# A 3-tap convolution as transforms and matmuls: from 6 products per 4 outputs to 8 products per 6

## The chip, the cores and the metric

The kernel runs on one NeuronCore of one Trainium2 chip (trn2). The metric is device time in microseconds (us), the median of the runs of a kernel; less is better. Some runs fall in a slower state and are labelled slow (here, over 1.5% above the fastest run of the same kernel). Ratios are taken over fast runs alone; a median is over all runs given, which includes one slow run of the changed kernel and one of the experiment `e9_w0late`. The span that a profile prints is about 2 us shorter than the time reported for the same run (before the change: spans of 207.6 to 208.5 us for times of 209.4 to 210.3 us). Stages below are told in span time, totals in reported time.

Engines: PE is TensorE's matmul, PEld its weight load, DVE is VectorE, ACT is ScalarE, POOL is GpSimd, SP the engine that issues the DMAs; a q after a name (SPq, ACTq) is that engine's sequencer. PSUM is the memory that the matmuls write, in eight banks of 512 fp32 values per partition; the other tiles lie in SBUF. The drain is the end of a run, when TensorE has little left to do: in the kernel before it is counted from 203.4 us, after the last full products, in the changed kernel from the end of the last unit's tail (below), with two products still to come.

## The reference

A 1-D convolution of three taps with padding, a batch norm with given statistics, and Silu. Everything is bf16 in memory.

```python
B, S, C = 2, 2048, 1024; K = 3
xp = jnp.pad(x, ((0, 0), (1, 1), (0, 0)))
y = sum(jnp.einsum('bsc,cd->bsd', xp[:, k:k + S, :], w[k]) for k in range(K))
inv_std = 1.0 / jnp.sqrt(var + 1e-5)
y = (y - mean) * (g * inv_std) + b
return _silu(y)            # (2, 2048, 1024)
```

## The kernel before

Both kernels avoid three full matmul passes, one per tap. A block of neighbouring outputs along `s` is computed from a linear transform of its inputs (`T`), one matmul product per transformed point against transformed weights, and a linear combination of the products. Before, a block has 4 outputs and 6 products, 1.5 multiplications per output where the plain form has 3.

The input transform is itself a small matmul: a window of x (up to 128 rows of `s`) is the stationary operand and a matrix of 6 points for 31 blocks is the moving one. The result goes from PSUM to SBUF as bf16.

```python
WT = 31                                    # blocks per window
for bi in range(B):
    for wi in range(NWIN):                 # 17 windows per batch
        nc.sync.dma_start(out=xw[...], in_=x[bi, lo:hi_ld + 1, :])
        for h in range(CT // CH):
            for c4 in range(CH):
                nc.tensor.matmul(grp[:, c4, 0:6 * ntile], lhsT=xw[0:kk, ct * P:(ct + 1) * P],
                                 rhs=Rm[0:kk, :, 0:ntile], start=True, stop=True)
            # 744 elements per partition, on ScalarE or VectorE by a running balance
            ev = nc.scalar.copy(dst, src)  # or nc.vector.tensor_copy(dst, src)
```

GpSimd makes the transformed weights of one chunk of 128 output channels: six sums and two scalings of 1,024 elements per partition. There are 8 chunks.

```python
nc.gpsimd.tensor_tensor(g32, w0, w2, op=ALU.add)
nc.gpsimd.tensor_tensor(uch[:, 0], g32, w1, op=ALU.add)
nc.gpsimd.tensor_tensor(uch[:, 1], g32, w1, op=ALU.subtract)
nc.gpsimd.tensor_scalar(w2x4, w2, 4.0, 0.0, op0=ALU.mult, op1=ALU.add)
nc.gpsimd.tensor_scalar(w1x2, w1, 2.0, 0.0, op0=ALU.mult, op1=ALU.add)
nc.gpsimd.tensor_tensor(f32, w0, w2x4, op=ALU.add)
nc.gpsimd.tensor_tensor(uch[:, 2], f32, w1x2, op=ALU.add)
nc.gpsimd.tensor_tensor(uch[:, 3], f32, w1x2, op=ALU.subtract)
```

Then come 16 units (8 chunks times 2 halves of the blocks, 512 blocks each). A unit is 48 matmuls of 512 columns, 10 VectorE operations, 2 ScalarE copies and 4 Silus. Each output row of the block has a contiguous row in `yT`; a DMA transpose and four strided stores bring it out. The last unit is cut in two halves that are transposed on TensorE, to keep the end short.

```python
for gidx, j in enumerate([1, 2, 3, 4, 0, 5]):
    for ct in range(CT):
        nc.tensor.matmul(M[j], lhsT=lhsT, rhs=T_sb[:, ct, j, nsl], start=(ct == 0), stop=(ct == CT - 1))
    if j == 1:
        nc.scalar.copy(S1, M[1])
    elif j == 2:
        nc.vector.tensor_tensor(bp, S1, M[2], op=ALU.subtract)
        nc.vector.tensor_tensor(M[2], S1, M[2], op=ALU.add)
    # ... likewise for the other products, then
    # nc.scalar.activation(yT[:, i, :], src, ACT.Silu, bias=beta[...], scale=sk[...])
```

## Time and profile before

| | before |
|---|---|
| median | 209.96 us (16 runs, 209.45 to 211.96) |
| load and transform stage | until 36.9 us |
| products | 36.9 to 203.4 us |
| drain | 6.2 us |

The profile was taken in a run of 211.4 us, a little above the median. The head of its page: the span, the busy time of each engine, and then tenths busy in 40 equal slices of the span, with the granted TensorE clock and the DMA engines' share.

```profile
span 209.6 us, 3041 instructions
...
PE 194.8 (93%) x1089; PEld 105.7 (50%) x1104; DVE 130.9 (62%) x225; ACT 95.9 (46%) x142; POOL 124.1 (59%) x83
...
PE   1998698999999999999999999999999999999980
...
PEclk9999979999999999999999999999999999999996
DMA  5999970892626963695359545965694545454562
...
```

TensorE is busy 93% of the span. The first six slices are different from the rest: the DMA row is full, the PE row has holes. The view by stretches of time makes a table of it. Its columns are the stretch, its length, then the busy us (and the number of instructions) of PE, PEld, DVE, ACT and POOL, then the granted clock, the DMA share and GB/s.

```profile
...
5.00:36.90 31.90, 27.69 (x270) 24.32 (x269) 26.39 (x31) 26.53 (x37) 13.18 (x8) 0.95 0.83 270
38.00:48.35 10.35, 10.30 (x49) 4.69 (x49) 5.58 (x10) 2.69 (x4) 9.52 (x14) 1.00 1.05 154
60.00:180.00 120.00, 119.42 (x547) 54.41 (x557) 70.39 (x115) 46.31 (x69) 86.92 (x48) 1.00 0.67 135
203.40:209.60 6.20, 0.79 (x8) 0.45 (x8) 1.95 (x7) 1.64 (x4) 0.00 (x0) 0.74 0.30 70
...
```

In the third row TensorE is busy 119.4 of 120 us while VectorE is busy 70, ScalarE 46 and GpSimd 87: the middle is TensorE's. The second row is one unit of 48 matmuls in 10.35 us, so 215.7 ns each.

The groups of instructions, kept apart by shape: line, engine, operation, tiles, shape, count, then busy us and the mean ns of one.

```profile
...
L316 PE MATMUL ps_all<-T_sb,uch 128*128 128x512 bf16 x466 | 105.3, 379 | 0.9
...
L306 ACT ACTIVATE yT<-y,beta,sk 128x512 bf16<-128x512 f32 x60 | 45.6, 806 | 58.5 <-DVE y L327 46.3 <-DVE y L337 12.2
...
L155 POOL TENSOR_TENSOR uch<-g,wch 128x1024 bf16<-128x1024 f32 x8 | 17.1, 2134 | 0.2
...
L321 DVE TENSOR_TENSOR ps_all<-S,ps_all 128x512 f32<-128x512 f32 x15 | 10.3, 689 | 0.0
...
```

The mean duration of a pipelined matmul (379 ns) is not its rate (215.7 ns), so rates are read from stretches.

### The profile page before, as it was taken

How to read it: one execution, taken by the hardware profiler on the slowest of the kernel's cores; microseconds unless marked ns; L12 is line 12 of the kernel's file. 1: busy time of each engine (PE TensorE's matmuls, PEld its weight loads, DVE VectorE, ACT ScalarE, POOL GpSimd, SP SyncE). 2: the span in 40 equal slices, each digit the busy share in tenths (PEclk: the TensorE clock that was granted, in tenths of full speed). 3: DMA queues.
4: the chain of work that ended last, by engine and by line, in shares of the span. 5: the costliest groups of instructions: out<-in, count | busy, mean ns of one | idle time of the engine just before them, and what ended most of it. 6: DMA issues, size and time to landing. Idle time of an engine off the chain costs nothing.

```text
span 209.6 us, 3041 instructions
## 1 busy us (share of the span) xinstructions
PE 194.8 (93%) x1089; PEld 105.7 (50%) x1104; DVE 130.9 (62%) x225; ACT 95.9 (46%) x142; POOL 124.1 (59%) x83
## 2 busy tenths in 40 slices
PE   1998698999999999999999999999999999999980
PEld 1977587444444444444444444444444444445870
DVE  6799579355656565647474747473838383829671
ACT  3799589234343343343434342424243434343651
POOL 3030299989999999839944994299659920000000
PEclk9999979999999999999999999999999999999996
DMA  5999970892626963695359545965694545454562
GB/s 180 373 340 288 348 276 2 87 214 54 152 57 145 212 140 68 142 213 130 76 132 227 119 86 133 177 159 95 146 208 104 100 100 100 100 103 100 102 142 60
DMA packets 96035, 31.40 MB, mean 150 GB/s; under 512 B 91606, under 2 KB 91606, under 8 KB 96020
## 3 DMA queue, kind: packets, MB, share of 16 engines
q1 hardware_dynamic: 95812, 30.42, 65.1%
q0 software_dynamic: 208, 0.79, 1.5%
q8 instruction: 8, 0.13, 0.2%
q14 instruction: 7, 0.06, 0.1%
HBM read 14.95 MB, written 8.39 MB: 111 GB/s over the span
## 4 chain that ended last, share of the span: by engine, by line
PE 69%; DMA 13%; POOL 5%; DVE 4%; ACT 4%; issue 2%; SPq 1%; ACTq 0%; DVEq 0%; POOLq 0%
PE ps_all L316 64%; DMA xw<-in_x_dram 8%; PE ps_all L205 5%; DMA wch<-in_w_dram 3%; ACT T_sb L217 3%; DMA o_sb<-yT 2%; POOL f L159 1%; POOL g L154 1%; POOL uch L156 1%; POOL uch L155 1%; SPq L247 1%; DVE Rm L82 1%; ACT yT L306 1%; DVE E L68 1%; DVE y L337 1%
## 5 line engine op out<-in xcount | busy, mean ns | idle before, releaser
L316 PE MATMUL ps_all<-T_sb,uch 128*128 128x512 bf16 (+1 forms) x530 | 112.9, 366 | 0.9
L316 PEld LDWEIGHTS <-uch 128*128 128x128 bf16 x544 | 53.1, 98 | 57.6 <-issue 0.3
L306 ACT ACTIVATE yT<-y,beta,sk 128x512 bf16<-128x512 f32 (+1 forms) x68 | 49.9, 781 | 62.5 <-DVE y L327 49.9
L316 PE MATMUL ps_all<-T_sb,wch 128*128 128x512 bf16 (+1 forms) x271 | 57.8, 366 | 0.1
L316 PEld LDWEIGHTS <-wch 128*128 128x128 bf16 x272 | 26.6, 98 | 28.7
L205 PE MATMUL ps_all<-Rm,xw 126*128 126x186 bf16 (+1 forms) x272 | 28.4, 261 | 8.4 <-DVE Rm L82 4.3
L320 DVE TENSOR_TENSOR bp<-S,ps_all 128x512 f32<-128x512 f32 (+1 forms) x17 | 11.2, 656 | 37.3 <-PE ps_all L316 31.6
L205 PEld LDWEIGHTS <-xw 126*128 126x128 bf16 (+1 forms) x272 | 25.0, 106 | 11.6 <-issue 8.0
L217 ACT CAST T_sb<-ps_all 128x744 bf16<-128x744 f32 (+1 forms) x37 | 26.9, 785 | 8.1 <-PE ps_all L205 7.7
L219 DVE CAST T_sb<-ps_all 128x744 bf16<-128x744 f32 (+1 forms) x31 | 26.7, 904 | 6.2 <-PE ps_all L205 5.9
L325 DVE TENSOR_TENSOR cp<-S,ps_all 128x512 f32<-128x512 f32 (+1 forms) x17 | 11.1, 656 | 29.9 <-PE ps_all L316 29.8
L323 ACT COPY S<-ps_all 128x512 f32<-128x512 f32 (+1 forms) x17 | 9.5, 560 | 35.4 <-PE ps_all L316 35.4
L154 POOL TENSOR_TENSOR g<-wch 128x1024 f32<-128x1024 bf16 x8 | 17.0, 2123 | 12.2 <-DMA wch<-in_w_dram 11.7
L158 POOL TENSOR_SCALAR w1x<-wch 128x1024 bf16<-128x1024 bf16 x8 | 8.4, 1045 | 19.3 <-DMA wch<-in_w_dram 19.1
L159 POOL TENSOR_TENSOR f<-wch,w2x 128x1024 f32<-128x1024 bf16 x8 | 17.0, 2128 | 0.4
L155 POOL TENSOR_TENSOR uch<-g,wch 128x1024 bf16<-128x1024 f32 x8 | 17.1, 2134 | 0.2
L160 POOL TENSOR_TENSOR uch<-f,w1x 128x1024 bf16<-128x1024 f32 x8 | 17.1, 2132 | 0.2
L156 POOL TENSOR_TENSOR uch<-g,wch 128x1024 bf16<-128x1024 f32 x8 | 17.1, 2133 | 0.0
L161 POOL TENSOR_TENSOR uch<-f,w1x 128x1024 bf16<-128x1024 f32 x8 | 17.1, 2132 | 0.0
L326 DVE TENSOR_TENSOR ps_all<-S,ps_all 128x512 f32<-128x512 f32 (+1 forms) x17 | 11.2, 658 | 0.0
L321 DVE TENSOR_TENSOR ps_all<-S,ps_all 128x512 f32<-128x512 f32 (+1 forms) x17 | 11.2, 658 | 0.0
L331 DVE SCALAR_TENSOR_TENSOR y<-ps_all,bp 128x512 f32<-128x512 f32 (+1 forms) x17 | 11.1, 650 | 0.0
(34 smaller groups left out, 89.1 us busy)
## 6 DMA issues: line engine op xcount, KB each, us to landing
xw<-in_x_dram SPq DMA_DIRECT2D x30, 256.0 KB, 5.9
out_dram<-o_sb SPq DMA_DIRECT2D x60, 128.0 KB, 2.2
wch<-in_w_dram SPq DMA_DIRECT2D x21, 256.0 KB, 4.2
wch<-in_w_dram POOLq DMA_DIRECT2D x1, 768.0 KB, 11.6
out_dram<-o_sb SPq DMA_DIRECT2D x8, 64.0 KB, 1.7
xw<-in_x_dram SPq DMA_DIRECT2D x2, 252.0 KB
xw<-in_x_dram SPq DMA_DIRECT2D x2, 130.0 KB
o_sb<-yT SPq DMA_TRANSPOSE x15, 4.3
```

The costliest lines, as they stand in the source:

```text
L154: nc.gpsimd.tensor_tensor(g32, w0, w2, op=ALU.add)
L155: nc.gpsimd.tensor_tensor(uch[:, 0], g32, w1, op=ALU.add)
L156: nc.gpsimd.tensor_tensor(uch[:, 1], g32, w1, op=ALU.subtract)
L159: nc.gpsimd.tensor_tensor(f32, w0, w2x4, op=ALU.add)
L160: nc.gpsimd.tensor_tensor(uch[:, 2], f32, w1x2, op=ALU.add)
L161: nc.gpsimd.tensor_tensor(uch[:, 3], f32, w1x2, op=ALU.subtract)
L205: nc.tensor.matmul(grp[:, c4, 0:6 * ntile], lhsT=xw[0:kk, ct * P:(ct + 1) * P], rhs=Rm[0:kk, :, 0:ntile], start=True, stop=True,)
L217: ev = nc.scalar.copy(dst, src)
L219: ev = nc.vector.tensor_copy(dst, src)
L306: nc.scalar.activation(yT[:, i, :], src, ACT.Silu, bias=beta[:, dc:dc + 1], scale=sk[:, dc, i:i + 1])
L316: nc.tensor.matmul(M[j], lhsT=lhsT, rhs=T_sb[:, ct, j, nsl], start=(ct == 0), stop=(ct == CT - 1))
L320: nc.vector.tensor_tensor(bp, S1, M[2], op=ALU.subtract)
```

## The change

The change takes 6 outputs per block and 8 products: 1.33 multiplications per output instead of 1.5. A batch has 342 blocks, which is also the width of a product, so a unit is one batch of one chunk: 64 matmuls of 342 columns. There are other differences:

- The instruction order on each engine is now as written, not chosen by a scheduler.
- Batch 2's transform is interleaved with the first products, instead of coming before them.
- The scalings of the weights move to ScalarE, and one of three first sums to VectorE, from chunk 2 on. A unit's products come in three parts: the head (four), the tail (two) and the two end rows.
- The end rows (0 and 5) are accumulated in PSUM by the last two products, on top of what VectorE wrote there, and finished during the next unit.
- `yT` now holds the output in its final order, block by block with 6 elements each. So Silu writes every sixth element (end rows) or runs of four (the other rows). One DMA transpose and one 512 KB store per unit follow, with no special last unit.

```diff
-WT = 31
+R = 6
+NJ = 8
+WT = 21
+    NB = -(-S // R)                                  # 342 blocks per batch
...
+        by_dve = q == 0 and dc > 1
+        e = epool.tile([P, CT, P], FP32, name="e0" if by_dve else "e")
+        (nc.vector if by_dve else nc.gpsimd).tensor_tensor(e, a, c, op=ALU.add)
+        nc.gpsimd.tensor_tensor(u[:, 0], e, o, op=ALU.add)
+        nc.gpsimd.tensor_tensor(u[:, 1], e, o, op=ALU.subtract)
...
-                nc.tensor.matmul(M[j], lhsT=lhsT, rhs=T_sb[:, ct, j, nsl], start=(ct == 0), stop=(ct == CT - 1))
+            nc.tensor.matmul(
+                ps[:, bank, 0:NB], lhsT=lhsT, rhs=T_sb[:, ct, j, nsl],
+                start=fresh and ct == 0, stop=ct == CT - 1, skip_group_check=not fresh,
+            )
+            between()                                # batch 2's transform, 3 jobs per 2 matmuls
...
+            stt(z[:, 0], s2, -0.0125, s1)            # head: 4 products, 10 VectorE operations
+            stt(y[:, 1], s2, -0.05, s1)
+            # ... z[:, 1], y[:, 0], y[:, 2], y[:, 3] likewise
...
+            emit_product(cp, self.dc, self.bi, 5, True, between)      # tail: 2 products, 8 operations
+            pc = self.copy(cp)
+            if prev:
+                prev.silu(prev.yT[:, :, 1:5], prev.y.rearrange("p i n -> p n i"))
+            emit_product(cm, self.dc, self.bi, 6, True, between)
+            # ... d3 and s3 in PSUM, then
+            stt(s3, s3, -1.6, z[:, 0])
+            stt(d3, d3, -0.05, z[:, 1])
+            self.yT = ypool.tile([P, NB, R], BF16, name="yT")
...
+        def ends(self, between):                                      # after the next unit's head
+            emit_product(cm, self.dc, self.bi, 0, False, between)
+            self.silu(self.yT[:, :, 0], ps[:, cm, 0:NB])
+            emit_product(cp, self.dc, self.bi, NJ - 1, False, between)
+            self.silu(self.yT[:, :, R - 1], ps[:, cp, 0:NB])
...
+            nc.sync.dma_start_transpose(out=o, in_=flat)
+            nc.sync.dma_start(out=out_v[self.bi, :, :, self.dc * P:(self.dc + 1) * P], in_=o)
...
+    for i, (dc, bi) in enumerate(seq):
+        unit = Unit(dc, bi, (4, 5) if i < 2 or i % 2 else (6, 7))
+        unit.head(between, prev)
+        if prev:
+            prev.ends(between)
+        # ... weight loads and sums of chunk dc + 2
+        unit.tail(between, prev)
+        if prev:
+            prev.store()
```

## The prediction

> **What bounds the kernel now.** TensorE, in three stages. (1) Load and input transform, 4.3 to 36.9 us: the view by stretches shows the DMA share at 1.0 or more until about 30 us; the chain of waits has 16 us of x loads here. TensorE runs in pieces. (2) Products, 36.9 to 203.4 us: each stretch of 10.35 us has 48 matmuls of 512 columns and 10.30 us of busy TensorE, so 215.7 ns per matmul; 256-column ones take about 109 ns. The Trainium skill, "TensorE: Matmul & The Clock Gate", section "Wait — 56ns, not 53.3ns?", gives columns / 2.4 GHz + 2.5 ns for a warm array; this trace agrees with both. VectorE is about 60% busy, ScalarE 40%, GpSimd up to 95%. (3) Drain, 203.4 to 209.6 us.
>
> **What the change does.** It goes from 6 products per 4 outputs to 8 per 6, so 1.5 to 1.33 columns per output: 1,024 matmuls of 342 columns instead of 768 full-size ones of 512. At 342/2.4 + 2.5 = 145 ns that is 148.8 us instead of 166.5 us: 17.7 us less on the critical path. Weight loads grow from 816 to 1,024, but a 128-column load fits under 145 ns as it fits under 109 ns now.
>
> It interleaves the second batch's transform with the first products, so x loads of batch 2 are hidden. Evacuations go from 744 to 504 elements; spaced 755 ns (ScalarE) and 884 ns (VectorE) now, I estimate 555 and 634 ns. 49 per batch, 27 and 22, is about 15 us of both engines per batch. So the first batch is done at about 21 us and the second at about 37.5 us, with 33 product matmuls already done. Then 991 x 145.3 ns = 144 us brings the last product to about 182 us, if nothing else binds.
>
> **Will another engine bind?** Two units (one weight chunk) take 18.6 us of TensorE.
> - VectorE: 18 operations of 342 per unit instead of 10 of 512. Back-to-back spacing is 597 ns at 512 and 331 ns at 256, so about 420 ns at 342: 7.6 us per unit, plus about 1.2 us for a weight sum in every second unit: 16.3 of 18.6 us. Tight, but it fits.
> - GpSimd: 8 operations of 2.13 us: 17.1 of 18.6 us; the scalings move to ScalarE.
> - ScalarE: about 11 of 18.6 us.
> - Chunk 1 has the whole transform on GpSimd (22 us per chunk, starting near 9 us), ready near 56 us, just when its last products start: I allow 0 to 3 us of stall.
>
> **Worse:** the drain. No split last unit and no TensorE transposes: eight VectorE operations (3.4 us), a last product and Silu (about 2 us), then a DMA transpose (4.3 us until stores start now) and a 512 KB store (about 3.5 us). About 11.5 us after the last product's slot, against 6.2 us.
>
> **Sum.** 182 + 11.5 + about 2.5 of stalls: 196 us, range 190 to 204. Faster by over 2%: 0.88; within 2%: 0.09; slower: 0.03.
>
> **What would show it.** Product spacing near 145 ns with TensorE over 98% busy between 60 and 180 us; VectorE about 85 to 90%, GpSimd about 90% there; transform of batch 2 over by 36 to 40 us; 11 to 14 us from the last tail product to the end.
>
> **What would make it wrong.** VectorE or GpSimd binding: VectorE runs in order, and waits for copies or for the weight sum would leave TensorE waiting for its PSUM banks; GpSimd and VectorE slowing each other where both read SBUF; ScalarE's strided four-row Silu being far slower than 1.43 us; TensorE cold in the interleaved stage (at the start of this trace four 186-column matmuls take 620 ns, half speed).

## The result, and the profile after

| | before | after |
|---|---|---|
| median | 209.96 us (16 runs) | 202.67 us (11 runs, 202.13 to 205.43) |
| ratio of the fast runs | | 0.9646, 95% interval 0.9612 to 0.9681 |

A ratio is the mean time of one kernel's fast runs over that of the other's in the same rounds, so it is not quite the ratio of the medians. The change is 3.5% faster. The result lies in the predicted range of 190 to 204 us, near its upper edge, and 6.7 us above its centre of 196 us.

The first profile of the changed kernel fell on its slowest run (205.43 us, span 203.3 us). The kernel was run again unchanged, and the profile of that run (202.82 us) is the one shown and compared from here on.

> The changed kernel again, unchanged, beside the others of this call, for a profile in the fast state (the first fell in the slow one): 202 to 203.5 us, the first stages ending about 3 us earlier than in the first profile.

The repeat gave 202.81 us, ratio 0.9695 (0.9639 to 0.9751). The first transform stage and the interleaved one ended 2.6 us earlier than in the slow profile (the first stretch of uninterrupted products starts at 39.41 us, not 42.04 us); after that the two profiles run alike.

The head of its page:

```profile
span 200.7 us, 3607 instructions
...
PE 176.1 (88%) x1296; PEld 123.1 (61%) x1296; DVE 164.8 (82%) x357; ACT 148.1 (74%) x172; POOL 155.2 (77%) x85
...
PE   2599788897999999999999999999999999995800
...
DVE  5469778999797999799799999998998979797200
...
PEclk9999999999999999999999999999999999999665
DMA  5999999650059846977696679469966266453593
...
```

The view by stretches, with the same columns as before; the second row is one unit, 64 matmuls at the predicted rate:

```profile
...
5.00:39.40 34.40, 28.65 (x297) 25.10 (x296) 26.21 (x45) 27.21 (x57) 29.61 (x18) 1.00 0.99 272
60.00:69.30 9.30, 9.30 (x66) 6.21 (x64) 7.84 (x19) 7.34 (x8) 9.14 (x6) 1.00 0.95 200
60.00:180.00 120.00, 120.00 (x829) 80.20 (x827) 110.83 (x239) 97.54 (x95) 104.51 (x48) 1.00 0.72 148
183.20:200.70 17.50, 4.16 (x16) 2.09 (x15) 3.56 (x8) 7.23 (x4) 0.00 (x0) 0.67 0.58 126
...
```

In the middle TensorE is busy all of the 120 us. VectorE went from 70 to 111 of 120 us, ScalarE from 46 to 98, GpSimd from 87 to 105: the spare time of all three is much smaller, but TensorE still sets the pace. The last row is the drain: 17.5 us, where the kernel before took 6.2 us and the prediction counted 13.8 us (11.5 us after the last product's slot, which includes two products of 1.16 us).

The groups by shape:

```profile
...
L218 PE MATMUL ps<-T_sb,u 128*128 128x342 bf16 x768 | 119.1, 307 | 3.5 <-ACT T_sb L209 1.9 <-ACT yT L287 1.6
...
L287 ACT ACTIVATE yT<-y,beta,scale 128x1368 bf16<-128x1368 f32 x16 | 44.5, 2782 | 1.2 <-issue 1.2
L287 ACT ACTIVATE yT<-ps,beta,scale 128x342 bf16<-128x342 f32 x32 | 42.6, 1508 | 21.9 <-PE ps L218 20.0 <-POOL u L149 1.9
...
L150 POOL TENSOR_TENSOR u<-e,w1x 128x1024 bf16<-128x1024 f32 x16 | 37.1, 2319 | 0.0
...
L148 DVE TENSOR_TENSOR e<-wch 128x1024 f32<-128x1024 bf16 x6 | 11.4, 1896 | 0.0
...
```

The Silus stand out: 1,508 ns for 342 elements, where a Silu of 512 elements took 806 ns before. VectorE's weight sum takes 1,896 ns where the prediction had 1.2 us, and the GpSimd operations beside it 2,319 ns instead of 2,132 ns.

The chain that ended last, in order of time (start, length, what):

```profile
...
50.59 132.53 PE ps L218 x912
...
186.47 4.07 ACT yT L287 x2
190.54 1.13 ACTq L385
```

From 50.59 us to 183.12 us the chain is TensorE alone: 912 matmuls in 132.53 us, 145.3 ns each. It is the predicted rate to the digit. The chain printed ends with Silu; what follows it, the transpose and the store, is in the timeline below.

The timeline of the drain (start, length, engine, line, operation, tiles, and in brackets the idle time before it and what ended it):

```profile
...
183.21 0.52 DVE L275 TENSOR_TENSOR ps<-pc,ps 128x342 f32<-128x342 f32 x1 [1.05 <-PE ps L218]
...
185.60 4.16 PE L218 MATMUL ps<-T_sb,wch 128*128 128x342 bf16 x16 [2.50 <-DVE ps L225]
...
186.30 0.51 DVE L225 SCALAR_TENSOR_TENSOR ps<-ps,z 128x342 f32<-128x342 f32 x1
186.47 2.71 ACT L287 ACTIVATE yT<-y,beta,scale 128x1368 bf16<-128x1368 f32 x1 [1.25 <-issue]
189.07 2.60 ACT L287 ACTIVATE yT<-ps,beta,scale 128x342 bf16<-128x342 f32 x2
...
191.70 2.01 SPq L300 DMA_TRANSPOSE o<-yT  x1
196.01 0.38 SPq L301 DMA_DIRECT2D out_dram<-o  x1
```

The drain is one thing after another: VectorE 3.3 us until the Silu starts, the four-row Silu 2.6 us until the next one starts, two end rows 2.6 us, 4.3 us from the issue of the transpose to that of the store, 4.7 us from there to the end.

### The profile page after: what moved, and what is told of

Its sections match the earlier page's. It is cut to its first block, busy times and chain, and to the rows that moved or that the text cites. A ratio compares the mean times of both kernels' runs of the same rounds, so it can differ in the third digit from the quotient of the medians.

```text
span 203.3 us, 3607 instructions
## 1 busy us (share of the span) xinstructions
PE 175.3 (86%) x1296; PEld 122.3 (60%) x1296; DVE 166.7 (82%) x357; ACT 147.8 (73%) x172; POOL 153.3 (75%) x85
## 4 chain that ended last, share of the span: by engine, by line
PE 65%; ACT 2%; DVE 1%; issue 1%; ACTq 1%; DVEq 0%
PE ps L218 65%; ACT yT L287 2%; ACTq L385 1%; DVE ps L275 0%; DVE y L225 0%; DVE ps L276 0%; DVEq L385 0%; DVE ps L225 0%; DVEq L275 0%
## 5 line engine op out<-in xcount | busy, mean ns | idle before, releaser
L218 PE MATMUL ps<-T_sb,u 128*128 128x342 bf16 x768 | 119.8, 308 | 2.9 <-ACT yT L287 1.6
L218 PEld LDWEIGHTS <-u 128*128 128x128 bf16 x768 | 74.7, 97 | 38.0 <-issue 2.5
L287 ACT ACTIVATE yT<-ps,beta,scale 128x342 bf16<-128x342 f32 x32 | 42.6, 1507 | 21.9 <-PE ps L218 21.9
L287 ACT ACTIVATE yT<-y,beta,scale 128x1368 bf16<-128x1368 f32 x16 | 44.3, 2769 | 1.3 <-issue 1.3
L218 PE MATMUL ps<-T_sb,wch 128*128 128x342 bf16 x256 | 39.9, 307 | 2.5 <-DVE ps L225 2.5
L150 POOL TENSOR_TENSOR u<-e,w1x 128x1024 bf16<-128x1024 f32 x16 | 37.1, 2321 | 0.0
L201 PE MATMUL ps<-rm,xw 128*128 128x168 bf16 (+1 forms) x256 | 28.4, 258 | 9.9 <-DMA xw<-in_x_dram 5.1
L209 ACT CAST T_sb<-ps 128x504 bf16<-128x504 f32 (+1 forms) x56 | 27.2, 567 | 12.1 <-PE ps L201 11.2
L149 POOL TENSOR_TENSOR u<-e,w1x 128x1024 bf16<-128x1024 f32 x16 | 35.0, 2189 | 1.3
L211 DVE CAST T_sb<-ps 128x504 bf16<-128x504 f32 (+2 forms) x42 | 25.6, 640 | 12.0 <-PE ps L201 11.5
L225 DVE SCALAR_TENSOR_TENSOR y<-ps,y 128x342 f32<-128x342 f32 x64 | 29.7, 506 | 0.6
L149 POOL TENSOR_TENSOR u<-e,wch 128x1024 bf16<-128x1024 f32 x8 | 17.1, 2132 | 2.6 <-PE ps L218 2.4
L150 POOL TENSOR_TENSOR u<-e,wch 128x1024 bf16<-128x1024 f32 x8 | 17.1, 2133 | 0.0
```

What stands on the lines that cost most here:

```text
L149: nc.gpsimd.tensor_tensor(u[:, 0], e, o, op=ALU.add)
L150: nc.gpsimd.tensor_tensor(u[:, 1], e, o, op=ALU.subtract)
L201: nc.tensor.matmul(v[:, c], lhsT=xw[0:rows, (c0 + c) * P:(c0 + c + 1) * P], rhs=rm[0:rows, :, 0:n], start=True, stop=True)
L209: nc.scalar.copy(dst, v)
L211: nc.vector.tensor_copy(dst, v)
L218: nc.tensor.matmul(ps[:, bank, 0:NB], lhsT=lhsT, rhs=T_sb[:, ct, j, nsl], start=fresh and ct == 0, stop=ct == CT - 1, skip_group_check=not ...
```

## The experiments

All were run with three rounds beside the kernel before, on three chips: `e1`, `e3`, `e4` and `e5` in one, the repeat with `e2`, `e6` and `e7` in the next, `e8` to `e11` in the last. The changed kernel's own ratio was 0.9646 and, in its repeat, 0.9695; a difference of half a per cent is not to be read. The repeat's fast runs also spread from 202.7 to 205.0 us. So a difference of 1 to 2 us from the repeat rests on the profiles as much as on the times.

### Does Silu's strided write explain the missing time?

Theory: Silu is slow because it writes every sixth bf16 element, and this costs time only where Silu is on the chain, at unit 1's PSUM banks and in the drain. Rivals: Silu is slow for another reason, or ScalarE limits the middle too. The experiment gives a wrong result: each of the six rows is written contiguously, and the DMA transpose carries the same bytes.

```diff
-                prev.silu(prev.yT[:, :, 1:5], prev.y.rearrange("p i n -> p n i"))
+                prev.silu(prev.yT[:, 1:5, :], prev.y)
...
-            self.yT = ypool.tile([P, NB, R], BF16, name="yT")
+            self.yT = ypool.tile([P, R, NB], BF16, name="yT")
...
-            self.silu(self.yT[:, :, 0], ps[:, cm, 0:NB])
+            self.silu(self.yT[:, 0, :], ps[:, cm, 0:NB])
...
```

> Wrong result on purpose: Silu writes each of the six output rows contiguously (layout row, block) instead of every sixth element; all else, and the bytes moved, are as after the change. Theory S (the strided write makes Silu slow, and it counts only at unit 1's PSUM wait and in the drain): one-row Silu falls from 1.51 to about 0.6 us, four-row from 2.77 to about 1.45 us; TensorE's wait of 1.6 us near 52 us falls under 0.7 us, the drain shortens by about 3 us; total 3.5 to 4.5 us less, near 198.5 us. Rival (Silu is slow for another reason, PSUM source or size): durations stay, time the same. Rival (ScalarE also limits the middle): more than 6 us less.

Measured: 201.47 us, ratio 0.9577 (0.9527 to 0.9628), span 198.7 us; wrong output. The groups by shape:

```profile
...
L287 ACT ACTIVATE yT<-y,beta,scale 128x1368 bf16<-128x1368 f32 x16 | 24.5, 1530 | 2.6 <-issue 2.6
...
L287 ACT ACTIVATE yT<-ps,beta,scale 128x342 bf16<-128x342 f32 x32 | 20.3, 636 | 30.7 <-PE ps L218 30.6
...
```

The durations are as expected: 1,508 became 636 ns and 2,782 became 1,530 ns, so the layout is what makes Silu slow. For the end rows, read from PSUM in order in both kernels, it is the write alone. For the four-row Silu the edit changes two things, as its diff shows: it also reads `y` row by row instead of jumping between rows. Which of the two costs the 1.25 us there is not shown. The Trainium skill, "ScalarE: Activation LUTs", section "What ACT_TABLE_LOAD costs", gives 186 ns, plus 93 ns for each per-partition operand, plus 0.833 ns per element. With two such operands an estimate from these figures is 657 ns for 342 elements and 1,512 ns for 1,368; the contiguous form agrees within 4%, the strided one does not at all.

TensorE's wait before unit 1's tail fell from 1.63 to 0.72 us, about as expected. The middle did not move, so ScalarE does not limit it. But the drain shortened by 1.3 us (17.5 to 16.2 us), not 3, and the total by 1.3 us against the repeat (2.0 us of span between the two profiles), not 3.5 to 4.5. So the layout explains only part of the missing time. The drain's timeline shows where the rest of the gain went:

```profile
...
184.94 3.97 PE L218 MATMUL ps<-T_sb,wch 128*128 128x342 bf16 x16 [2.50 <-DVE ps L225]
...
187.42 0.64 ACT L287 ACTIVATE yT<-ps,beta,scale 128x342 bf16<-128x342 f32 x1
...
188.95 0.64 ACT L287 ACTIVATE yT<-ps,beta,scale 128x342 bf16<-128x342 f32 x1 [0.90 <-PE ps L218]
189.61 2.58 SPq L300 DMA_TRANSPOSE o<-yT  x1
...
```

The last 16 matmuls took 3.97 us, 248 ns each instead of 145, and the last Silu waited 0.90 us for them. The three Silus together became 2.4 us shorter here (5.2 to 2.8 us), and this wait took back 0.9 of it. TensorE had paused 2.5 us for VectorE, and the granted clock in the stretch from 185 to 190 us was 0.70. In the kernel as changed the same slow products are hidden behind the slow Silu (4.16 us, granted clock 0.66, from 185.60 us above). Taking one link out of a serial chain uncovered the next: TensorE running at a reduced clock.

### Is the cost per 4-byte word?

From 1,508 ns for 342 elements and 2,782 ns for 1,368 one might guess a cost per 4-byte word touched: three words for the four middle rows, one for an end row. Moving the tile by one element makes it two aligned words for the middle rows.

```diff
-            self.yT = ypool.tile([P, NB, R], BF16, name="yT")
+            self.yS = ypool.tile([P, NB * R + 2], BF16, name="yT")
+            self.yT = self.yS[:, 1:NB * R + 1].rearrange("p (n i) -> p n i", i=R)
...
```

> Correct result: the tile that Silu writes starts one bf16 element later, so that rows 1 to 4 of each block fill two aligned 4-byte words instead of touching three. Theory W (the cost is per 4-byte word touched, about 2.4 ns): four-row Silu falls from 2.77 to about 2.0 us, one-row stays 1.5 us; about 0.7 us less in all, if the DMA transpose does not mind the odd start. Theory E (the cost is per element written out of sequence): both stay, time the same.

Measured: 202.92 us, ratio 0.967 (0.9604 to 0.9735), correct. The four-row Silu took 2,762 ns, the one-row 1,506 ns: nothing moved. The word theory falls. What exactly the cost counts stays open; 0.9 us (end row) to 1.3 us (four rows) per Silu is what the layout costs.

### Does unit 1 wait for unit 0's banks?

Units 0 and 1 use the same two PSUM banks for their last products. In the repeat's timeline this is the line of TensorE that waits:

```profile
...
50.59 7.12 PE L218 MATMUL ps<-T_sb,u 128*128 128x342 bf16 x48 [1.63 <-ACT yT L287]
...
```

```diff
-        unit = Unit(dc, bi, (4, 5) if i < 2 or i % 2 else (6, 7))
+        unit = Unit(dc, bi, (6, 7) if i % 2 else (4, 5))
```

> Correct result: units take their last two PSUM banks in turn from the start, so unit 1 no longer writes the banks that unit 0's end rows still hold. Theory: TensorE's wait of 1.63 us on the one-row Silu before 53 us (a strided Silu of 1.5 us, where the prediction counted 0.6) vanishes whole, 1.3 to 1.7 us less. Rival: VectorE is busy without a gap there, so the wait only moves to a PSUM bank that VectorE holds: under 0.5 us.

Measured: 201.61 us, ratio 0.9603 (0.9576 to 0.9629), correct; the repeat of the change in the same rounds had 202.81 us and 0.9695. So 1.2 us by the medians. In its profile TensorE goes from 47.44 us to the end of unit 1 without that wait:

```profile
...
49.76 7.12 PE L218 MATMUL ps<-T_sb,u 128*128 128x342 bf16 x48
...
```

VectorE, busy without a gap in that stretch, does not take it back.

### Can the drain be cut?

The last unit alone is finished in two halves of 171 blocks, transposed on TensorE and stored in four pieces, as the kernel before did.

```diff
-    prev.silu(prev.yT[:, :, 1:5], prev.y.rearrange("p i n -> p n i"))
-    prev.ends(between)
-    prev.store()
+    prev.drain(between, CUTS)
+        def drain(self, between, cuts):
+            for lo, hi in cuts:                       # (0, 171), (171, 342)
+                self.silu(self.yT[:, lo:hi, 1:5], self.y[:, :, lo:hi].rearrange("p i n -> p n i"))
+                emit_product(cm, self.dc, self.bi, 0, False, between, lo, hi)
+                self.silu(self.yT[:, lo:hi, 0], ps[:, cm, lo:hi])
+                # ... row 5 likewise
+            for q in range(4):
+                for k in range(4):
+                    nc.tensor.transpose(v[:, k], flat[:, (4 * q + k) * P:(4 * q + k + 1) * P], ident)
+                # ... copy to o, store a quarter
```

> Correct result: the last unit alone is finished in two halves of 171 blocks, transposed on TensorE and stored in four pieces, instead of whole rows, a DMA transpose and one 512 KB store. Theory (the drain of 17.5 us is a serial chain after the last tail product: VectorE 3.3, four-row Silu 2.7, end rows 2.6, DMA transpose 4.3, store 4.5 us): the drain falls to 11.5 to 13 us, 4.5 to 6 us less. Rival (the end is held by what is still in the DMA queues, unit 14's transpose and store): under 2 us.

Measured: 199.38 us, ratio 0.95 (0.9474 to 0.9526), correct: 3.4 us less than the repeat. The drain is 14.5 us (183.3 to 197.8 us). This is less than expected. The timeline offers one reason, which the run after the next tests: TensorE started the first half's end rows only when VectorE was nearly done with the second half, and then ran at a granted clock of 0.66 to 0.70.

```profile
...
187.02 4.22 PE L221 MATMUL ps<-T_sb,wch 128*128 128x171 bf16 x32 [3.81 <-DVE ps L228]
...
```

With the banks in turn as well:

> Correct result: the banks in turn and the halved drain together. If both theories hold and the two places are independent, the gains add: 6 to 7.5 us less than the change, 195 to 197 us. If they hand back to another engine, less than the sum.

Measured: 197.31 us, ratio 0.9411 (0.9389 to 0.9434), correct: 5.5 us less than the repeat. The two gains were 1.2 and 3.4 us, so they add, within the noise; both were smaller than I had expected, so the sum missed its window of 195 to 197 us by little.

Then each half got PSUM banks of its own. The Trainium skill, "PSUM — Partial Sum Buffer", section "PSUM bank collisions raise a hardware error", says to guard PSUM by bank and 32-partition quadrant (in the simple version by bank), not by address, and a program that follows this makes halves of one bank wait for each other.

```diff
-    CUTS = ((0, NB // 2), (NB // 2, NB))
+    CUTS = ((0, NB // 2, 6, 7), (NB // 2, NB, 0, 2))
...
```

The lines cut here also issue that unit's two tail products and their copies by halves.

> Correct result: as e7_both, but the two halves of the last unit use PSUM banks of their own. In e6_drain TensorE waited 3.81 us for VectorE before the end rows, that is until the second half's combination had written the bank, not only the first's. Theory (halves in one bank wait for each other): the end rows of the first half start 1.5 to 2 us earlier, the drain falls from 14.5 to about 12.5 us, 195 to 196 us in all. Rival (the two Silu in a row before it hold the chain anyway): under 0.7 us.

```profile
...
181.90 1.48 PE L221 MATMUL ps<-T_sb,wch 128*128 128x171 bf16 x16 [1.01 <-DVE ps L228]
...
183.97 1.48 PE L221 MATMUL ps<-T_sb,wch 128*128 128x171 bf16 x16 [0.59 <-DVE ps L228]
...
186.85 1.48 ACT L295 ACTIVATE yT<-ps,beta,scale 128x171 bf16<-128x171 f32 x2
187.61 0.38 SPq L326 DMA_DIRECT2D out_dram<-o  x1
188.04 3.72 SPq L319 DMA_DIRECT2D out_dram<-o  x4
...
```

The wait of 3.81 us became 1.01 and 0.59 us, TensorE stayed at full clock, and Silu was done at 188.3 us, some 7.5 us after the last tail product instead of 9.6 us in e7_both. But the time is 196.76 us, ratio 0.9382 (0.931 to 0.9453), 0.5 us better at most: the two runs are from different calls and their intervals overlap, and between the profiles the drain fell only from 14.5 to 14.0 us. So the wait for the bank was not by itself what kept the drain above its expected length. From the last Silu to the end it is 6.6 us now, and was 4.9 us in e7_both: the four stores are issued over 3.72 us, behind unit 14's 512 KB store that was issued at 187.61 us. So the theory of the banks holds for TensorE, and by this timeline the gain was handed to the DMA queue, which was the rival in e6_drain. The total lies where the expectation had put its own rival (under 0.7 us), but the Silus, which that rival blamed, did end 2.1 us earlier after the tail; no run isolates the queue. This is the lowest median measured: 6.2% under the kernel before.

### What did the interleaving bring?

```diff
     between = Between()
+    for job_n, job in enumerate(between.jobs):
+        t_job(job, (job_n + 1) % 8)
+    between.jobs = []
```

> Correct result: all of batch 2's transform is emitted before the first product, so nothing is interleaved. If the interleaving hides the loads as the prediction counted it (33 products done for free), this is 4 to 5 us slower than the change. If the stage is so held by loads that interleaving gains nothing, it is within 1.5 us of it.

Measured: 206.8 us, ratio 0.9847 (0.9792 to 0.9902): 4.0 us slower than the repeat, 4.1 us slower than the change's median. This is near the predicted worth of 33 products done while x is loaded (33 x 145 ns is 4.8 us). The profile shows the same shift: the unbroken chain of 912 products starts 3.9 us later than in the repeat (50.59 us) and is as long.

```profile
...
54.47 132.53 PE ps L218 x912
...
```

About half of the change's gain over the kernel before would be lost without it.

### What holds the first stages?

TensorE idles near 8 us and, in the slow profile, 2.2 us near 28 us, both times for x and after the issue of weight loads. Two experiments move the weight loads.

```diff
-    load_w(1)                       # after six windows of batch 2
     for wi in order[6:]:
         load_x(1, wi)
+    load_w(1)
```

> Correct result: weight chunk 1 is loaded after all x of batch 2, not after its sixth window. Theory D (the second transform stage is held by x that waits behind the 256-byte rows of weight chunk 1, and TensorE then runs cold): TensorE's 2.2 us of idling near 28 us and the half clock after it vanish, the stage ends near 38 us instead of 41.8 us; GpSimd starts chunk 1 some 4 us later, which may hand part of it back; total 1 to 3 us less. Rival (the stage is bound by the evacuations): it still ends at 41 to 42 us, time the same or longer.

Measured: 205.74 us, ratio 0.9799 (0.9736 to 0.9861): about 3 us slower. The wait near 28 us is gone, but in a fast run it is only 0.7 us to begin with, and the interleaved stage ended at 37.9 instead of 39.4 us. The gain of 1.5 us was more than lost to GpSimd, as TensorE's waits show:

```profile
...
60.66 1.33 PE L218 MATMUL ps<-T_sb,u 128*128 128x342 bf16 x8 [1.90 <-POOL u L149]
62.73 7.30 PE L218 MATMUL ps<-T_sb,u 128*128 128x342 bf16 x40 [0.75 <-POOL u L150]
...
```

The sums for chunk 1 came too late, and TensorE waited for them. After the waits its granted clock was 0.60 from 62.7 to 66.2 us, and these 40 products took 7.0 us instead of 5.8 us. The theory of the loads held in direction but not in size, and it was the smaller effect.

```diff
-        if i == 2:
+        if i == 7:
             load_w(0)
+            # in unit 0, chunk 1's three scalings, now:
+            scale_w(1, 2, 4.0, nc.vector)
```

> Correct result: e8_halves, with weight chunk 0 loaded after the eighth window of x, not the third, and chunk 1's three scalings on VectorE. Theory (the first stage stands still 2.3 us near 8 us behind the weights' 256-byte rows, and restarts cold): the stage ends 1.5 to 2 us earlier and the gain reaches the end, because GpSimd's chunk 1, which would be late, is 3.1 us shorter. Rival (GpSimd's chain of 22 us per chunk from the arrival of chunk 0 sets the start of chunk 1's products, as in e3_w1late): same or slower than e8_halves.

Measured: 198.91 us (four runs, one of them slow), ratio 0.9433 (0.9353 to 0.9514), against 196.76 us and 0.9382 for e8_halves; the intervals overlap, so no gain, perhaps a loss. The stall did not vanish: it moved from 7.4 us to 11.2 us and was again 2.21 us long, and the first product still started at 21.5 us. So moving chunk 0's load later does not free the first stage. Its DMA share is full until it ends, and the bytes of batch 1 and chunk 0 must all have arrived: that is argued from this and from the DMA row, not shown by a run with fewer bytes.

### How close are VectorE and GpSimd?

One VectorE operation per unit is done three times; the result is the same.

```diff
-            stt(z[:, 1], d2, -0.4, d1)
+            stt(z[:, 1], d2, -0.4, d1)
+            stt(z[:, 1], d2, -0.4, d1)
+            stt(z[:, 1], d2, -0.4, d1)
```

> Correct result: the changed kernel with one VectorE operation of each unit done three times, 0.84 us more per unit. VectorE is busy 92% of the middle (8.6 of 9.3 us per unit). If the middle is bound by TensorE alone with VectorE that close, VectorE now needs 9.44 us and binds: TensorE no longer 100% busy, 1.5 to 3.5 us more in all. If VectorE has more slack than that: under 1 us more. If VectorE already bound (the prediction's worry): about 13 us more.

```profile
...
60.00:180.00 120.00, 117.41 (x804) 77.74 (x802) 117.95 (x256) 96.75 (x92) 101.03 (x48) 1.00 0.71 143
...
```

Measured: 207.35 us, ratio 0.9873 (0.9798 to 0.9948): 4.5 us slower than the repeat, a little more than expected. VectorE is busy 117.95 of 120 us and TensorE is no longer full, with waits for VectorE of 0.26 us in every chunk late in the run. So VectorE was not binding before, and it is less than 0.84 us per unit away from it.

The other one puts the first sum of every chunk back on GpSimd:

```diff
-        by_dve = q == 0 and dc > 1
+        by_dve = False
```

> Correct result: the changed kernel with the first weight sum of every chunk on GpSimd, none on VectorE. GpSimd then has nine operations of 2.13 us, 19.2 us per chunk, where TensorE takes 18.6 us. If GpSimd is as close to binding as that: chunks come later and later, 1 to 4 us more in all. If the earlier chunks have stock: the same time. VectorE's busy share of the middle falls by about 5 points, and GpSimd's stretched operations (2.32 us) return to 2.13 us.

```profile
...
135.87 5.98 PE L218 MATMUL ps<-T_sb,u 128*128 128x342 bf16 x40 [0.76 <-POOL u L150]
...
155.42 5.98 PE L218 MATMUL ps<-T_sb,u 128*128 128x342 bf16 x40 [0.76 <-POOL u L150]
...
174.97 5.98 PE L218 MATMUL ps<-T_sb,u 128*128 128x342 bf16 x40 [0.76 <-POOL u L150]
...
```

Measured: 204.93 us, ratio 0.9747 (0.9689 to 0.9806): 2.1 us slower. Its interval overlaps the repeat's, so the profile carries this point. From 135.87 us on, TensorE waits for the weights in every chunk, and a chunk takes 19.55 us instead of 18.6 us. GpSimd's operations are 2,140 ns again instead of 2,319 ns. The Trainium skill, "GPSIMD Engine Reference", section "8. Key points", says that GpSimd shares its SBUF interfaces with VectorE and that VectorE instructions with two SBUF inputs contend; the weight sum is the only such operation on VectorE in the middle, and these runs agree with it.

## Why the prediction was right

Point by point, with the repeat's profile (200.7 us of span).

- **The product rate.** Predicted 145.3 ns per matmul, measured 145.3 ns over 912 of them, with TensorE busy 120.0 of 120 us in the middle. Right. This is the whole gain of the change on paper: 17.7 us. By the two profiles (209.6 and 200.7 us of span) about half of it was left. The drain without its two products took back 9.0 us (15.2 against 6.2 us) and the stall 1.6 us, while the first stages without the 32 products done in them became 2.1 us shorter (34.8 against 36.9 us).
- **No other engine binds.** Right, and as close as it was put: VectorE measured 92% where 85 to 90% was predicted, GpSimd 87% (about 90%), ScalarE 81% (59%). The two experiments above show that two more VectorE operations per unit, or one more GpSimd sum per chunk, bind.
- **Interleaving.** Predicted to save 33 products, 4.8 us; removing it cost 4.0 us. Right. The stage itself ended some 2 us later than counted: 32 products were done at 39.41 us, where the prediction had 33 at 37.5 us. The first product started at 22.03 us, about 1 us late, and the interleaved part took about 1 us longer than counted.
- **Stalls.** Allowed 2.5 us, mostly for GpSimd's chunk 1. The measured stall is 1.63 us and is another one, unit 1's PSUM banks held by the strided Silu. GpSimd's chunk 1 was just in time, as the experiment with the late load shows.
- **The drain.** This is the term that was mis-sized: "About 11.5 us after the last product's slot", so 13.8 us after the last tail product, against 17.5 us measured. The item at fault is "a last product and Silu (about 2 us)": from the start of the four-row Silu to the end of the last end row it took 5.2 us. Contiguous, these three Silus would last about 2.8 us (1,530 + 2 x 636 ns); in the run with contiguous rows this stretch took 3.8 us, with the wait for TensorE. So the layout explains 1.4 us of the 3.2 us here; the rest is that the four-row Silu was left out of the items, and the wait for TensorE. The store to the end took 4.7 us, not 3.5. The prediction had named "ScalarE's strided four-row Silu being far slower than 1.43 us" among what would make it wrong, but it priced the contiguous form, and its list of the drain's items has no four-row Silu.
- **The unit of the sum.** The prediction added stages read from a trace and compared the sum with reported times. Those are about 2 us longer than the spans, so 196 us of span is about 198 us reported. This slip is 2 us of the 6.7 us by which the centre missed.

The sum: 2.0 us in the first stages, 3.7 us in the drain, minus 0.9 us of stalls that did not come, gives 4.8 us of span (measured: 200.7 against 196, 4.7 us). With the 2.1 us between span and reported time this accounts for the 6.7 us. Only the stalls erred the other way, so it was not a cancelling of errors that kept the result in the range; the range was wide enough, by 1.3 us.

The mis-sizing in the middle did no harm because TensorE hides it: Silus of twice the length and a weight sum of 1.9 us instead of 1.2 us fit below 9.3 us per unit.

## What to carry to other kernels

A change that trades matmul columns for elementwise work pays only until the next engine is full: count every engine's operations per unit against the new, shorter unit, as here VectorE at 92% and GpSimd at 87% are the end of this road. Price operations in the layout that the new code writes, not in that of the old trace: the same Silu took 0.64 us contiguous and 1.51 us with every sixth element. Slow operations that hide in the middle come back in the drain, where everything is serial; there a gain in one link is soon taken by the next (by the timelines here the TensorE clock, then the DMA queue), so the whole chain has to be reshaped.

## What the Trainium skill lacked or had wrong

- "ScalarE: Activation LUTs": nothing on strided writes. The runs show 1,508 ns instead of 636 ns for 342 elements at a step of 6 bf16, and 2,782 ns instead of 1,530 ns for 342 runs of four (where the order of the read changed too). "SBUF — State Buffer", section "Door 1: The DMA port swizzle", says that up to 8 bf16 can be strided without cost; at a step of 6 ScalarE's write was not free here. (The same paragraph asks for two hits per 16-byte line; a step of 12 bytes gives 1.33. No run here tells whether that is the reason.) Shifting the start by 2 bytes changed nothing (2,762 ns).
- "TensorE: Matmul & The Clock Gate", section "What's actually happening": the clock falls after an idle window of about 3.4 us. Here a shorter pause was often enough. After the pause of 2.50 us in the drain, the 16 matmuls of 342 columns took 3.58 to 4.16 us in seven fast profiles (224 to 260 ns each; granted clock 0.66 from 185 to 190 us in the repeat), but 2.58 us after the same pause in the slow first profile and in the fast one of the run with VectorE's operation done three times. In the slow first profile a pause of 2.17 us near 28 us was followed by a clock of 0.50 from 30.06 to 33.40 us.
- "GPSIMD Engine Reference", section "8. Key points": names the contention between GpSimd and a VectorE instruction with two SBUF inputs, without a size. Here a VectorE sum of 1,024 elements took 1.6 to 2.3 us (means of the kernels; 1.2 to 2.8 us singly in the repeat), and the slowest group of GpSimd sums in the repeat 2,319 ns on average, against 2,140 ns without that VectorE sum. Singly, such a GpSimd sum took 2.13 us, and about 3.1 us once per chunk, beside VectorE's sum.
